# A three-stage attention and feed-forward kernel, rewritten around a list schedule of its own

## The chip, the cores and the metric

The kernel runs as one program on one core of one Trainium2 chip. The metric is the device time of one execution in microseconds (us). A core has five engines that run side by side, each through its own queue in order: TensorE (PE, matrix products, with its weight loads shown as PEld), VectorE (DVE), ScalarE (ACT), GpSimd (POOL) and SyncE (SP, which issues the transfers here).

## The reference

Four batches pass through three stages. All arithmetic is in float32 and the answer must be near a float32 result.

```
A  8 heads of 64; 32 global and 512 local positions (S = 544):
   out_g = softmax(q_g k_all^T / 8) v_all
   out_l = softmax([q_l k_g^T / 8, q_l k_l^T / 8 where |i-j| <= 32]) [v_g; v_l]
   x = heads side by side                                  (544 x 512)
B  4 experts, each a causal attention of one head of 64:
   top 2 of x w_gate, softmax over the two = gate
   out = sum_e gate_e * softmax_causal(x wq_e (x wk_e)^T / 8) (x wv_e) wo_e
C  h = relu(out w_in); c = 3-tap convolution of h along the sequence
   result = (h * sigmoid(c)) w_out                         (544 x 512)
```

(The sequence of stages B and C is the 544 positions; `w_in`, `w_out` and `conv_w` arrive as 64-bit floats that the kernel decodes itself.)

## The kernel before

Where more than float32r's precision is wanted, the kernel splits an operand into a high and a low part (`split`, `sub`, `sub_pool`) and makes three products of them, high by high, high by low and low by high. `wo` is multiplied into `w_in` once (`fold_gen`, L196), so stage C starts from the heads' outputs `oh`, `ol`.

**Stage A** (`stream_a`) takes two heads at a time. K and Q of a head stand on 64 partitions twice; K is split into `k1`, `k2` on POOL (L91, L94) and Q on ACT and DVE (L277, L278). Global scores go over 544 keys (`scores_g`, L291); local scores go by 128 queries against windows of 192 or 224 keys (`scores_l`, L312). DVE adds a mask and takes the maximum (L317), ACT makes the exponential and its sum (L322), DVE the reciprocal, and POOL multiplies the probabilities by it (L91, tile `Pa`). They are transposed on PE (`trans_l`, L346), copied by ACT (L347), and multiplied by V on PE into two halves of 64 output rows (`pv_a`, L361; global queries L371). The result is split into `xh`, `xl`.

**Stage B** (`phase_b`) projects Q, K (L444) and V with the gate's logits (L457), ranks the gates on DVE, then works through eight items (expert pair `p`, query tile `i`): `scores` (L541, and the causal mask as a bf16 product, L543), maximum on DVE (L546), exponential with sum on ACT (L548), scaling on POOL (L555), `trans` (L565, copied by DVE, L567), `pv` (L576). The last 32 queries of all four experts go together (L504, L523, L590).

**Stage C** (`phase_c`) makes `h` by columns of 128 (L621), then relu and the middle tap on ACT (L628, L631, L633), two taps on DVE (L641), tanh on ACT (L644), the product on DVE (L648), a split (L650, L104), and `project` (L661) in three products, 768 matrix products in all.

`decode` turns 64-bit weights into float32 with six DVE instructions of 256 columns for each piece (L110 to L119); there are 16 pieces each of `w_in` and `w_out`.

**What sets the order.** Three generators (A; B; C with the weights) are merged by rates, and the framework's own scheduler reorders the result:

```
merge([stream_a(), stream_b(), stream_c()], [60, 46, 36])
with tile.TileContext(nc, schedule_with_timeline_sim=True) as tc:
```

Of the kernel before, what the change touches and what calls it, by code (L numbers as in the profile page):

```python
# [19 lines left out]
S = SL + SG  # L20
KB = 608
# [5 lines left out]
WIN = [(0, 192), (128, 352), (256, 480), (384, 608)]  # L27

PIECE = [[(0, 128, 0), (128, 64, 1)], [(128, 128, 1), (256, 96, 2)],
         [(256, 128, 2), (384, 96, 3)], [(384, 96, 3), (480, 128, 4)]]  # L30
VCH = [(0, 128), (128, 128), (256, 128), (384, 96), (480, 128)]


def key_of_column():
    cols = [("g", t) for t in range(32)] + [("l", t) for t in range(256)]
    cols += [("g", t) for t in range(32)] + [("l", t) for t in range(256, 512)]
    return cols + [("g", t) for t in range(32)]


def local_mask():  # L40
    import numpy as np
    cols = key_of_column()
    m = np.zeros((128, 4, 224), np.float32)
    for i, (a, b) in enumerate(WIN):
        for c in range(a, b):
            kind, t = cols[c]
            if kind == "g":
                continue
            q = 128 * i + np.arange(128)
            m[:, i, c - a] = np.where(np.abs(q - t) <= 32, 0.0, BIG)  # L50
    return m
# [3 lines left out]
def body(ctx, tc, kq, vA, w_gate, wqk, wv, woT, w_in, conv_w, w_out, cmask, out):  # L55
# [7 lines left out]
    def T(shape, dt, name, bufs=1):  # L63
        return sb.tile(shape, dt, name=name, bufs=bufs)

    def PS(*shape):
        return ps.tile([128] + list(shape), F32, name="s", bufs=5)

    def PO(*shape):
        return ps.tile([128] + list(shape), F32, name="t", bufs=3)  # L70

    NW = 6
    NPA = 3
    LB, LS, L0 = (2, 4, 6), (2, 3, 6, 7, 10, 11), 4

    def W2(dt=F32, n=512):
        w = T([128, S], F32, "w2", NW)[:, :n]
        return w if dt == F32 else w.bitcast(dt)

    def W1(name, dt=F32):  # L80
        w = T([128, 274], F32, name, 3)
        return w if dt == F32 else w.bitcast(dt)

    NG = 8

    def G(name, dt=F32R):
        w = T([128, 272], F32, name, NG)
        return w if dt == F32 else w.bitcast(dt)
# [7 lines left out]
    def split(hi, lo, src, eng, scale=1.0):  # L96
        if eng is act:
            act.activation(hi, src, AF.Copy, scale=scale)
        else:
            scale_pool(hi, src, scale)  # L100
        dve.scalar_tensor_tensor(lo, src, scale, hi.bitcast(F32), op0=ALU.mult, op1=ALU.subtract)  # L101

# [3 lines left out]
    def decode(raw, w, dst=None):  # L106

        lo, up = raw[:, :, 0], raw[:, :, 1]
        t, f1, p, q = W1("hb", I32)[:, :w], W1("cv", I32)[:, :w], W1("hb", I32)[:, :w], W1("cv")[:, :w]
        dve.tensor_scalar(t, up, 3, 0x3FFFFFF8, op0=ALU.logical_shift_left, op1=ALU.bitwise_and)  # L110
        dve.scalar_tensor_tensor(f1, up, -0x40000000, t, op0=ALU.bitwise_and, op1=ALU.bitwise_or)
        dve.tensor_scalar(p, f1, -0x800000, None, op0=ALU.bitwise_and)
        dve.scalar_tensor_tensor(q, lo.bitcast(U32), 2.0 ** -52, p.bitcast(F32), op0=ALU.mult, op1=ALU.mult)
        dve.tensor_tensor(q, f1.bitcast(F32), q, op=ALU.add)  # L114

        e = W1("hb")[:, :w]
        act.activation(e, up.bitcast(F32), AF.Abs)
        dst = q if dst is None else dst
        dve.scalar_tensor_tensor(dst, e, GUARD, q, op0=ALU.is_ge, op1=ALU.mult)  # L119
        return dst  # L120
# [641 lines left out]
```

## Time and profile before

| | |
|---|---|
| time, median of 3 runs | 587.53 us (585.02 to 591.34) |
| span of the profiled execution, first to last instruction | 579.8 us |
| median of the runs less the span | 7.7 us |
| mean granted clock of TensorE over the span | 0.975 |
| busy: PE, PEld, DVE, ACT, POOL | 523.0, 454.3, 429.0, 357.3, 240.0 us |
| moved by DMA | 40.45 MB |

The profile records one execution from its first to its last instruction. The time of that execution as the runs are timed is not recorded beside it; what lies around the span is taken as the 7.7 us of the third row. Matrix products are pipelined and their recorded lengths overlap, so the pace of PE is read from one start to the next, not from busy time.

### The profile page before, as it was taken

The numbers are of one execution on the slowest core, as the hardware profiler recorded it, in microseconds if no ns is written. First come the engines' busy times: TensorE is split into PE (matmuls) and PEld (weight loads), VectorE is DVE, ScalarE is ACT, GpSimd is POOL, SyncE is SP. The second block draws the span as 40 slices with busy tenths as digits, with TensorE's granted clock in tenths as the row PEclk, the third lists the DMA queues.
The fourth block names the chain that finished last, engine by engine and source line by source line (L and its number), as shares of the span: only waits on it lengthen the run. The fifth ranks groups of instructions, "written<-read, shape, count | busy, mean of one in ns | idle before, by whom it ended". The sixth has DMA issues, their size and how long they took to land.

```text
span 579.8 us, 12650 instructions
## 1 busy us (share of the span) xinstructions
PE 523.0 (90%) x4392; PEld 454.3 (78%) x4392; DVE 429.0 (74%) x1316; ACT 357.3 (62%) x1112; POOL 240.0 (41%) x390
## 2 busy tenths in 40 slices
PE   2268888999889698999999999999999999999997
PEld 2157777897667688977777999887879998678997
DVE  4999999767789899869995646656782565485854
ACT  3567767647578567568965566465962663373864
POOL 6758867715666652247465600245402001222000
PEclk9989979999799899999998999999999999999999
DMA  8954444301434450022232400031100000000011
GB/s 215 295 160 112 137 132 111 81 3 42 104 97 128 110 156 1 21 75 52 69 96 56 125 12 2 11 95 53 35 2 20 20 2 21 10 11 11 31 40 38
DMA packets 19855, 40.45 MB, mean 70 GB/s; under 512 B 3408, under 2 KB 8912, under 8 KB 19792
## 3 DMA queue, kind: packets, MB, share of 16 engines
q1 hardware_dynamic: 19792, 39.65, 24.7%
q8 instruction: 34, 0.56, 0.4%
q14 instruction: 29, 0.24, 0.1%
HBM read 35.18 MB, written 4.46 MB: 68 GB/s over the span
## 4 chain that ended last, share of the span: by engine, by line
PE 59%; DVE 17%; DMA 8%; POOL 6%; issue 4%; ACT 3%; SPq 1%; ACTq 0%; POOLq 0%; DVEq 0%
PE s L661 16%; PE s L444 7%; DMA raw<-in_kq_dram 7%; PE s L621 6%; PE s L457 5%; PE t L361 4%; PE s L541 4%; PE t L576 3%; PE t L565 2%; PE s L312 2%; PE t L346 2%; POOL Pa L91 2%; DVE Pa L317 2%; DVE qs L278 2%; DVE cv L114 2%
## 5 line engine op out<-in xcount | busy, mean ns | idle before, releaser
L91 POOL TENSOR_SCALAR Pa<-Pa,ml 128x224 f32<-128x224 f32 (+1 forms) x128 | 70.0, 563 | 29.8 <-DVE ml L326 17.3
L641 DVE SCALAR_TENSOR_TENSOR cv<-hb,cw,cv 128x272 f32<-128x272 f32 x128 | 65.2, 525 | 12.4 <-ACT cv L633 10.8
L661 PE MATMUL s<-gl,wuh 128*128 128x272 f32 x256 | 73.7, 295 | 0.0
L661 PE MATMUL s<-gh,wul 128*128 128x272 f32 x256 | 72.5, 290 | 0.0
L661 PE MATMUL s<-gh,wuh 128*128 128x272 f32 x256 | 70.5, 300 | 0.0
L322 ACT ACTIVATE Pa<-Pa,ml 128x224 f32<-128x224 f32 (+1 forms) x128 | 59.7, 468 | 11.9 <-DVE ml L317 11.7
L555 POOL TENSOR_SCALAR w<-w,stB,gate 128x128 f32<-128x128 f32 (+3 forms) x64 | 45.0, 710 | 53.1 <-DVE stB L553 23.7
L361 PE MATMUL t<-PA,vr 128*64 128x128 f32 (+2 forms) x512 | 52.5, 290 | 2.8 <-ACT PA L347 2.6
L546 DVE TENSOR_REDUCE stB<-s 128x1 f32<-128x128 f32 (+3 forms) x64 | 30.8, 486 | 25.9 <-PE s L543 25.3
L317 DVE CUSTOM_DVE_ANT_0 Pa<-s,lmask 128x224 f32<-128x224 f32 (+1 forms) x128 | 43.9, 373 | 8.1 <-PE s L312 5.2
L347 ACT ACTIVATE PA<-t 128x512 f32<-128x512 f32 x64 | 37.5, 593 | 19.3 <-PE t L346 15.8
L661 PEld LDWEIGHTS s<-gl,wuh 128*128 128x128 f32 x256 | 48.7, 191 | 0.8 <-issue 0.5
L661 PEld LDWEIGHTS s<-gh,wul 128*128 128x128 f32 x256 | 48.5, 190 | 0.0
L661 PEld LDWEIGHTS s<-gh,wuh 128*128 128x128 f32 x256 | 46.4, 191 | 1.6 <-issue 1.2
L361 PEld LDWEIGHTS t<-PA,vr 128*64 128x64 f32 (+2 forms) x512 | 33.5, 138 | 16.2 <-issue 8.3
L346 PE MATMUL t<-ident,Pa 128*128 128x128 f32 x256 | 42.2, 292 | 1.3 <-POOL Pa L91 0.6
L444 PE MATMUL s<-xh,wqkh 128*128 128x272 f32 x128 | 38.7, 302 | 2.6 <-DVE kl L101 1.8
L567 DVE COPY w<-t 128x128 f32<-128x128 f32 (+3 forms) x64 | 30.2, 484 | 14.1 <-PE t L565 13.8
L548 ACT ACTIVATE w<-s,stB 128x128 f32<-128x128 f32 (+3 forms) x64 | 33.0, 522 | 11.8 <-DVE stB L546 7.8
L621 PE MATMUL s<-oh,wfh 128*128 128x274 f32 x128 | 38.9, 304 | 1.0 <-ACT hb L628 1.0
L94 POOL TENSOR_TENSOR k<-raw,k 128x608 fp32r<-128x608 f32 x24 | 38.1, 1586 | 1.4
L312 PE MATMUL s<-k,qs 128*128 128x192 f32 (+1 forms) x208 | 36.0, 306 | 2.5 <-DVE ml L317 2.2
(185 smaller groups left out, 1599.7 us busy)
## 6 DMA issues: line engine op xcount, KB each, us to landing
raw<-in_kq_dram SPq DMA_DIRECT2D x56, 288.0 KB, 4.2
vr<-in_vA_dram SPq DMA_DIRECT2D x16, 320.0 KB, 3.0
out_dram<-w SPq DMA_DIRECT2D x32, 136.0 KB, 1.8
w<-in_w_in_dram SPq DMA_DIRECT2D x16, 256.0 KB, 3.1
w<-in_w_out_dram SPq DMA_DIRECT2D x16, 256.0 KB, 3.9
vB<-in_kq_dram SPq DMA_DIRECT2D x6, 288.0 KB, 4.8
w<-in_wqk_dram SPq DMA_DIRECT2D x4, 256.0 KB, 4.8
w<-in_woT_dram SPq DMA_DIRECT2D x2, 256.0 KB, 5.4
```

The source lines that it names most:

```text
L91: pool.tensor_scalar(dst, src, s, 1.0, op0=ALU.mult, op1=ALU.mult)
L94: pool.tensor_tensor(lo, src, hi.bitcast(F32), op=ALU.subtract)
L312: pe.matmul(t[:, j, :width[i]], qs[:, 128 * i:128 * i + 128], kk[:, a:e], start=(k == 0), stop=(k == 1))
L317: dve.tensor_tensor_reduce(out=Pa[:, i, :w], in0=t[:, j, :w], in1=lmask[:, i, :w], scale=1.0, scalar=3e38, op0=ALU.add, op1=ALU.min, accum ...
L322: act.activation(Pa[:, i, :w], Pa[:, i, :w], AF.Exp, bias=ml[:, i:i + 1], scale=-1.0, accum_out=ml[:, 4 + i:5 + i])
L346: pe.transpose(t[:, 2 * j + p, :], Pa[:, i, c:c + 128], ident)
L361: pe.matmul(o[64 * y:64 * y + 64, i, :], vr[:r, v, 64 * y:64 * y + 64], PA[y, z][:r, 2 * j + p, :], start=(p == 0), stop=(p == 1))
L444: pe.matmul(acc[:, :272], wa[:, c, m], xa[c][:, s], start=(n == 0), stop=(n == 11))
L555: pool.tensor_scalar(PB[y][:, :w], PB[y][:, :w], st[:, 4 + y:5 + y], gate[:, i, 2 * p + y:2 * p + y + 1], op0=ALU.mult, op1=ALU.mult)
L621: pe.matmul(acc[:, :274], a[:, p, 128 * f:128 * f + 128], x[:, p, a0:a0 + 274], start=(k == 0), stop=(k == 5))
L641: dve.scalar_tensor_tensor(cv[:, :N], hb[:, o:o + N], cw[:, k, f:f + 1], cv[:, :N], op0=ALU.mult, op1=ALU.add)
L661: pe.matmul(acc[:, :N], w[:, f, sl], a, start=(f == 0 and k == 0), stop=(f == 7 and k == 2))
```

## The change

Nearly all of `body` is new. The names below are those of the new kernel.

* **An order of its own.** Each piece of work is an `op` with an engine, an assumed length, what it reads and writes, and a due time from a table `PLAN`. `Schedule.run` puts the ops of all five engines into one order (earliest start first, then due time; on PE an op of another tile shape is put back by `HOLD`) and gives out places in a few large tiles (`work`, `xg`, `kq`, `v`, `st`, and the eight PSUM banks `acc`). The framework keeps that order (`tc.manual_schedule`).
* **Stage A by 32 queries.** Each group of 32 local queries meets 128 keys (`local`). Heads are paired on the two halves of the partitions. Q K^T is one float32 product on a tile of 64 rows by 32 columns (512 products, L572), the mask a bf16 product behind each (512, L578), so eight groups share the array. K and Q are no longer split. The global scores use the same tiles (L639).
* **Sums by a column of ones.** V has a 65th column of ones, so P V also gives the softmax sum, and 64 columns are divided behind it (L617). ACT's sums, POOL's scaling of probabilities and the separate mask pass on DVE go; P V is turned round (output rows are queries: 512 products of 32x65, L607; 192, L667; stage B 160 of 128x65, L807), and the result needs another transposition (L625, L820).
* **Stage B** puts the two experts' products side by side on the two row halves (L782) with a mask of half height (L787).
* **Stage C in pairs.** Relu, tanh, product, split, copies and stores take two column blocks (544 columns) at a time; the middle tap goes from ACT to POOL.
* **Decode** takes 512 columns at a time; one of six DVE instructions goes to POOL.

Instructions by engine as ordered: PE products 3736 before (without weight loads), 4692 now; DVE 1316 and 699; ACT 880 and 588; POOL 393 and 255; SP transfers 165 and 97.

The core of the diff:

```diff
-    merge([stream_a(), stream_b(), stream_c()], [60, 46, 36])
+    order = sch.run(trace)
+    with tc.manual_schedule():
+        for o in order:
+            o.fn()
...
+PLAN = {"A": [(0, 26), (26, 75), (75, 170), (170, 265)],
+        "B": [(30, 80), (80, 175), (180, 275), (275, 350)],
...
+                p = c[1].prio
+                if e == "PE" and c[1].mode != mode:
+                    p += self.HOLD
...
+            for t in range(4):
+                for y in range(2):
+                    rows = slice(64 * y, 64 * y + 64)
+                    for g in range(4):
+                        j = 4 * t + g
+                        o = S_[y].ap()[32 * g:32 * g + 32, 128 * t:128 * t + 128]
+                        q = kb.ap()[rows, KB + 32 * j:KB + 32 * j + 32]
+                        pe.matmul(o, q, kb.ap()[rows, 32 * WIN[j]:32 * WIN[j] + 128], start=True, stop=False)
...
+                        pe.matmul(o, quart[rows], am[rows, which[j]], start=False, stop=True)
...
+            op("POOL", .25, lambda y=y: scale_pool(st[y].ap()[:, 4:8], st[y].ap()[:, 0:4], 0.125), r=[st[y]], w=[(st[y], 1)], tag="sclA")
...
+                        pe.matmul(ov()[32 * g:32 * g + 32, y, t], PT[y].ap()[:, 128 * t + 32 * g:128 * t + 32 * g + 32],
+                                  vv[y].ap()[:, 65 * n:65 * n + 65], start=True, stop=True)
...
+                for n, (a, k) in enumerate(((0, 0), (0, 1), (1, 0))):
+                    for y in range(2):
+                        rows = slice(64 * y, 64 * y + 64)
+                        pe.matmul(t.ap()[:, 512 * y:512 * y + w], Q[rows, a, p, qi], K[rows, k, p, :w], start=(n == 0), stop=False)
...
+                        pe.matmul(oe()[:, e], PT.ap()[:, 128 * j:128 * j + 128], vB[:, j, e, :], start=(j == 0), stop=(j == i))
...
+                op("ACT", t_act(544), lambda cv=cv: act.activation(cv.ap()[:, :544], cv.ap()[:, :544], AF.Tanh, scale=0.5), w=ct, tag="tanh")
```

Three places of the order. The first is PE in stage A. Before, where the second pair of heads begins (`s` and `t` are PSUM tiles, `Pg` and `Pa` probabilities):

```order
L291 MATMUL s<-k_121,qs_88 64x272 x2
L335 MATMUL t<-ident,Pg 128x64 x5
L346 MATMUL t<-ident,Pa_82 128x128 x8
L196 MATMUL s<-gl,oh 128x256 x2
L312 MATMUL s<-k_120,qs_88 128x192
L312 MATMUL s<-k_121,qs_88 128x192
L312 MATMUL s<-k_120,qs_88 128x224
```

Now, in the first batch (`acc` is PSUM, `kq` holds K and Q, `work` probabilities, `v` is V with its column of ones, `am` and `quart` make the mask):

```order
L639 MATMUL acc<-kq 32x512 x4
L639 MATMUL acc<-kq 32x192 x4
L594 MATMUL acc<-ident,work 128x128 x12
L654 MATMUL acc<-ident,work 128x128 x6
L607 MATMUL acc<-v,work 32x65 x32
L667 MATMUL acc<-v,work 32x65 x12
L572 MATMUL acc<-kq 32x128 x8
L578 LDWEIGHTS quart
L578 MATMUL acc<-am,quart 32x128
```

Products of one shape now stand in longer runs: eight global score products, 18 transpositions, 44 products of P V, and then a local score group, of whose four blocks the last rows begin the first (eight scores, then eight masks, each with its weight load).

The second place is PE in stage B of the last batch, at the widest query tile (512 keys). Before, one of its four score groups among stage C's products (`gl`, `gh`, `wuh`, `wul`):

```order
L661 MATMUL s<-gh,wuh 128x272
L541 MATMUL s<-kh,qh 128x512
L541 MATMUL s<-kl,qh 128x512
L541 MATMUL s<-kh,qlo 128x512
L543 LDWEIGHTS identb
L543 MATMUL s<-cm,identb 128x128
L565 MATMUL t<-ident,w_7028 128x128 x3
L661 MATMUL s<-gl,wuh 128x272
L661 MATMUL s<-gh,wul 128x272
L661 MATMUL s<-gh,wuh 128x272
```

Now, the score group of two experts (`k`, `q`), ahead of it two transpositions and the last 32 queries' P V:

```order
L867 MATMUL acc<-vB,work 32x65 x20
L800 MATMUL acc<-ident,work 128x128 x8
L877 MATMUL acc<-ident,work 128x128
L782 MATMUL acc<-k,q 128x512 x6
L787 LDWEIGHTS half
L787 MATMUL acc<-cm,half 128x128
```

The score products of two experts stand as one run of six with their masks (four, of which the first is shown) behind. Between matrix products of different tile shapes PE changes 357 times in the order before and 154 times now.

The third place is DVE in the opening. Before, where the first pieces of `w_in` are decoded (`hb`, `cv`):

```order
L110 TENSOR_SCALAR hb<-w_194 128x256
L111 SCALAR_TENSOR_TENSOR cv<-w_194,hb 128x256
L101 SCALAR_TENSOR_TENSOR wqkl<-w_303,wqkh 128x512
L112 TENSOR_SCALAR hb<-cv 128x256
L113 SCALAR_TENSOR_TENSOR cv<-w_194,hb 128x256
L114 TENSOR_TENSOR cv<-cv 128x256
L110 TENSOR_SCALAR hb<-w_307 128x256
L278 SCALAR_TENSOR_TENSOR qs_87<-vB,qs_87 64x544
L119 SCALAR_TENSOR_TENSOR cv<-hb,cv 128x256
L111 SCALAR_TENSOR_TENSOR cv<-w_307,hb 128x256
```

Now (`early` holds the pieces of `w_in`):

```order
L614 TENSOR_SCALAR st<-acc 128x8
L615 RECIPROCAL st<-st 128x8
L617 TENSOR_TENSOR work<-acc,st 128x4x64 x2
L671 TENSOR_SCALAR st<-acc 128x1
L672 RECIPROCAL st<-st 128x1
L674 TENSOR_SCALAR work<-acc,st 128x64 x2
L464 SCALAR_TENSOR_TENSOR early<-early 128x512
L452 TENSOR_SCALAR early<-early 128x512
L582 TENSOR_REDUCE st<-acc 128x4 x2
L337 TENSOR_TENSOR xg<-acc,xg 128x512
L337 TENSOR_TENSOR xg<-acc,xg 64x32 x4
L454 SCALAR_TENSOR_TENSOR early<-early 128x512
L456 TENSOR_SCALAR early<-early 128x512
```

The decode's steps are of 512 columns in place of 256, the addition is no longer among them, and they stand between the first heads' divisions (L614 to L617, L671 to L674) on DVE as before.

## Rows read from the trace of the kernel before

**Rows 1.** The page: its span, and part 1, TensorE's.

```profile
span 579.8 us, 12650 instructions
...
PE 523.0 (90%) x4392; PEld 454.3 (78%) x4392; DVE 429.0 (74%) x1316; ACT 357.3 (62%) x1112; POOL 240.0 (41%) x390
```

**Rows 2.** The page, part 4: the chain that ended last, by engine.

```profile
PE 59%; DVE 17%; DMA 8%; POOL 6%; issue 4%; ACT 3%; SPq 1%; ACTq 0%; POOLq 0%; DVEq 0%
```

**Rows 3.** Windows: length, busy us of each engine (x instructions), granted clock, DMA share, GB/s.

```profile
0.00:30.00 30.00, 8.01 (x36) 7.08 (x37) 21.64 (x41) 12.63 (x29) 20.42 (x34) 1.00 0.95 255
30.00:60.00 30.00, 23.15 (x168) 19.18 (x168) 28.80 (x99) 21.02 (x69) 20.06 (x25) 0.89 0.51 140
60.00:100.00 40.00, 34.39 (x314) 28.93 (x313) 37.68 (x114) 27.66 (x91) 31.19 (x40) 0.91 0.44 124
...
400.00:450.00 50.00, 49.60 (x444) 42.73 (x441) 33.46 (x95) 30.95 (x97) 15.52 (x31) 1.00 0.08 26
```

**Rows 4.** The chain in order of time: start, length, engine, tile, line, instructions.

```profile
537.38 0.88 PE t L565 x8
...
545.70 9.00 PE s L661 x72
...
563.82 11.30 PE s L661 x90
```

**Rows 5.** Timeline of TensorE near 505 and 515 us: start, length to the last end.

```profile
505.30 0.28 PE L621 MATMUL s<-oh,wfl 128*128 128x274 f32 x1
505.52 0.65 PE L576 MATMUL t<-w,vB 128*64 128x128 f32 x6
...
506.32 0.29 PE L621 MATMUL s<-ol,wfh 128*128 128x274 f32 x1
...
515.08 0.50 PE L541 MATMUL s<-kh,qh 64*128 64x512 f32 x1
515.42 0.39 PE L541 MATMUL s<-kl,qh 64*128 64x512 f32 x1
515.65 0.39 PE L541 MATMUL s<-kh,qlo 64*128 64x512 f32 x1
515.97 0.23 PE L543 MATMUL s<-cm,identb 128*128 128x128 bf16 x1
516.04 0.50 PE L565 MATMUL t<-ident,w 128*128 128x128 f32 x3
```

**Rows 6.** Timeline of TensorE from 318 to 323 us.

```profile
318.05 0.78 PE L371 MATMUL t<-PGT,vr 128*64 128x32 f32 x20
318.76 0.46 PE L291 MATMUL s<-k,qs 128*64 128x272 f32 x2
319.05 1.05 PE L312 MATMUL s<-k,qs 128*128 128x192 f32 x8
320.03 0.98 PE L361 MATMUL t<-PA,vr 128*64 128x128 f32 x13
...
320.86 1.14 PE L576 MATMUL t<-w,vB 128*64 128x128 f32 x15
321.93 0.71 PE L291 MATMUL s<-k,qs 128*64 128x272 f32 x4
322.57 0.52 PE L335 MATMUL t<-ident,Pg 64*128 64x64 f32 x5
323.02 1.09 PE L346 MATMUL t<-ident,Pa 128*128 128x128 f32 x8
```

**Rows 7.** Lines by form: busy us, mean ns of one, idle before and its releaser.

```profile
L641 DVE SCALAR_TENSOR_TENSOR cv<-hb,cw,cv 128x272 f32<-128x272 f32 x128 | 65.2, 525 | 12.4 <-ACT cv L633 10.8 <-ACT oh L592 0.3
...
L94 POOL TENSOR_TENSOR k<-raw,k 128x608 fp32r<-128x608 f32 x24 | 38.1, 1586 | 1.4
...
L361 PE MATMUL t<-PA,vr 128*64 128x128 f32 x256 | 44.1, 295 | 2.8 <-ACT PA L347 2.6 <-DMA vr<-in_vA_dram 0.2
...
L104 DVE TENSOR_TENSOR xl<-t,xh 128x512 fp32r<-128x512 f32 x16 | 10.9, 682 | 1.8 <-ACT xh L366 1.7
```

More of the change, by code (lines that the diff above doesn't have):

```diff
@@ new lines, with key_blocks, masks @@
+WIN = [0, 0, 2, 3, 4, 6, 7, 8, 10, 11, 12, 14, 15, 16, 18, 20]
+VW = sorted(set(WIN))
+def key_blocks():
+    out = []
+    for p in range(24):
+        if p % 4 == 0:
+            out.append(("g", 0))
+        elif p == 22:
+            out.append(("l", 14))
+        elif p == 23:
+            out.append(("z", 0))
+        else:
+            out.append(("l", 3 * (p // 4) + p % 4 - 1))
+    return out
+def masks():
+    import numpy as np
+    blocks = key_blocks()
+    found, which = [], []
+    for j, w in enumerate(WIN):
+        q = 32 * j + np.arange(32)
+        m, seen = np.zeros((32, 128), np.float32), set()
+        for c in range(4):
+            kind, t = blocks[w + c]
+            k = 32 * t + np.arange(32)
+            ok = np.zeros((32, 32), bool)
+            if kind == "g":
+                ok[:] = True
+            elif kind == "l":
+                ok = np.abs(q[:, None] - k[None, :]) <= 32
+            assert (kind, t) not in seen
+            seen.add((kind, t))
+            m[:, 32 * c:32 * c + 32] = np.where(ok, 0.0, -BIG)
+        assert (m == 0).sum() == 32 * 32 + sum(min(q1 + 32, SL - 1) - max(q1 - 32, 0) + 1 for q1 in q)
+        for n, f in enumerate(found):
+            if (f == m).all():
+                which.append(n)
+                break
+        else:
+            which.append(len(found))
+            found.append(m)
+    return found, which
@@ L467, in phase_b @@
+        op("POOL", .15, lambda: pool.memset(vB[:, :, :, 64:65], 1.0), r=[("lg", i) for i in range(5)], w=vtok + ["vBone"], tag="one")
+        gate = gates[b % 2]
+        ga, gb = gw
         le = lg[:, :, :, None].to_broadcast([128, 5, 4, 4])
@@ L715, in host_layout @@
+    constants()
+    stage_a(0)
+    fold()
+    constants2()
+    split_weights()
+    conv_load()
+    wout()
+    for b in range(NB):
+        if b:
+            stage_a(b)
+        if b:
+            stage_c(b - 1)
+        stage_b(b)
+    stage_c(NB - 1)
+    order = sch.run(trace)
+    if (tune or {}).get("DRY"):
+        early.close()
+        return sch
+    with tc.manual_schedule():
+        for o in order:
+            o.fn()
+    return sch
 def host_layout(inputs):
```

1343 lines of the change are left out of this document (759 added, 584 removed), and 2 rows, old and new, of the table PLAN.

## The prediction

> **What bounds the kernel now.** I read the page first. TensorE (PE) is busy 523.0 of 579.8 us, the others far less [rows 1], and the chain that ended last runs over PE for 59% of the span and DVE for 17% [rows 2]. The windows say when each counts. In the first 100 us PE is busy 8.01, 23.15 and 34.39 us and issues only 518 of its 4392 products (36, 168 and 314), while DVE is busy 28.80 of 30 us from 30 to 60 and the transfers fill the first 30 us (share 0.95, 255 GB/s). From 400 to 450 PE is busy 49.60 of 50 us [rows 3]. So it is an opening in which PE is starved, and then a long stretch that PE bounds; the last products end at 575.12 us, 4.7 us before the span does [rows 4]. In the long stretch the change is worth what it takes off PE's own time, which I therefore price by kind, from one start to the next.
>
> **Prices on PE.** The big products cost 9.00/72 = 0.125 us and a transposition of 128 columns 0.88/8 = 0.110 us [rows 4]. Plain float32 products go in two passes: L361 shows 256 records of 128 rows for 128 products [rows 7]. From 320.03 to 321.93 us stand 32 such passes of 128 columns (two records are missing): 0.06 us each, though one pass over 128 columns costs a transposition 0.110. So two tiles of 64 output columns run side by side [rows 6]. Passes of 32 columns in L371 cost 0.71/20 = 0.036 us, L312 0.98/8 = 0.122, L291 0.64/4 = 0.160, and a transposition of 64 columns (0.45 less half a shape change)/5 = 0.07 [rows 6]. Score products over 512 columns cost 0.23 us, the mask 0.07. A change of shape: from 505.30 to 506.32 us are two big steps (0.25), eight passes (0.44 at 0.055) and two changes, which leaves 0.165 us for each [rows 5].
>
> **The change part by part, on PE.** Before and after:
> - Big products (1824 at 0.125, and the fold, 96 of 256 columns or 48 of 512): 240 and 239 us. Nothing is gained.
> - Transpositions: 436 x 0.110 and 80 x 0.09 make 55; 464 x 0.110 make 51.
> - Scores of stage A: 128 x 0.160 and 256 x 0.122 make 51. Now there are 64 blocks of eight tiles, each two passes and a mask, 2 x 0.11 + 0.07 = 0.29 us if all eight run together. The trace shows two column tiles together, never two row halves (L541 takes one expert at a time [rows 5]). The ends are 64 x 0.29 = 18.6 us (all together) and 148 (one by one). If the columns go together and the halves do not, it is 37. I take 28, halfway between 18.6 and 37, since column tiles cost nothing where they are shown. The global scores (eight times, four tiles, passes of 512 and 192 columns, 0.59 us a pair) are 9.4 together, 19 with the halves apart and 38 one by one; I take 14. Together 42.
> - P V of stage A: 512 passes x 0.06 and 320 x 0.036 make 42. Now 1024 passes of 65 columns (0.07 each) by four tiles, 18, and 384 by two, 13: 31 in all. Only pairs are shown, so the upper ends are 36 + 13 = 49 in pairs and 99 alone.
> - Scores of stage B: 16 groups of each width, three products (0.23 at 512, less in proportion, not under 0.11) and a mask make 34. Now the same products in pairs and 128 half masks: 39 if the row halves do not overlap, 19 if they do; I take 29.
> - P V of stage B and of the last queries: 320 x 0.06 and 160 x 0.036 make 25. Now 320 x 0.07 (128 rows out, no tiles) and 160/4 x 0.07 make 25. Nothing is gained.
> - Changes of shape: 357 x 0.165 = 59 and 154 x 0.165 = 25.
>
> That is 506 before and 442 now. More than half of the saving of 64 us is the grouping by shape.
>
> **PE's own idle time.** Of the span before, 580 - 506 = 74 us are left. The opening's 518 products are 518/4392 x 506 = 60 us of work in 100, so 40 is lost there; 5 at the end; 29 of the 475 between, or 6%. The opening now: before stage C can use `w_out`, DVE must decode 16 pieces in five steps of 512 columns each, about 0.75 us by L104's 0.682 [rows 7], 60 us; two batches of stage A take it some 36 and stage B's first batch 22, 118 us in all. Two batches of stage A and all weights are about 24 MB, 95 us at 255 GB/s [rows 3]. In these 118 us PE can have the first two batches and part of the third of stage A, the fold and stage B's first batch, 95 to 110 us. I take 24 us lost (10 to 60). For the other 340 us I take 4.5%, 15 us, since the new order knows all engines at once, and 5 at the end. Idle 44.
>
> **The added waits.** Each maximum is now scaled on POOL before ACT can make the exponential (L582, L331, L587). ACT's queue is in order, and behind that exponential stand copies out of PSUM that later products wait for. POOL may be in a subtraction of 512 columns then, 1.3 us by L94's 1.586 for 608 [rows 7]. Twenty such hops lie in the opening: 0 to 26 us, covered by the 24; later POOL has little to do. The halved decode and the paired stage C cost nothing because DVE falls from 429 to about 330 us (128 x 0.525 for L641 [rows 7], 212 of some 512 columns at 0.70, the rest 115) and ACT to about 290, both well under PE.
>
> **Sum.** 442 + 44 = 486 us of span, and the 7.7 us between span and median: 494 us, against 587.53. The span before makes 587.5 in the same way, so the sum stands to the median as it does to the profile.
>
> **Rivals.**
> - *More overlap.* The row halves run side by side and the order holds: scores of A 28 for 42, of B 19 for 29, idle 30 for 44. 494 - 38 = 456. For it: column tiles overlap without loss [rows 6]. Against it: no two row halves in the trace.
> - *A price for each pass.* Small passes cost what L371's do, 0.036 us, whatever runs beside them: 1536 passes and masks of the local scores 55 for 28, 1024 of P V 36 for 18. 494 + 45 = 539. For it: L371's passes are a quarter as long as L361's and cost 0.036 against 0.06 [rows 6]. [...]
> - *The opening and the fixed order.* PE waits 60 us in the opening and 6% later as before: 494 + 36 + 5 = 535. For it: DVE's 118 us, and a granted clock of 0.89 and 0.91 where PE was fed badly [rows 3].
> - *Pairs only.* No more than two tiles together: scores of A 74 + 19 for 42, P V 49 for 31. 494 + 69 = 563.
> - *Slower than before.* The tiles of 64 by 32 run one after another, so that the rewriting does not do what it says: scores of A 148 + 38 for 42, 494 + 144 = 638. It decides from 94 us on: with the global scores as taken, when a block of eight tiles costs 1.9 us and not 0.44 (28/64). Against it: the pairs of rows 6. [...]
>
> **How the numbers follow.** The forecast has 0.42 (470 to 520), more overlap 0.18, a price for each pass 0.15, the opening 0.12, pairs only 0.06, slower 0.05, and 0.02 for no change. A measurement of this kernel can tell about 1% from no change. Faster is the sum of the first five, 0.93; the same 0.02; slower 0.05. The range goes from the best case to just short of pairs only, 455 to 560, and leaves out about 0.15.
>
> **What would show it.** Right: PE's records in runs of one shape; a local score group (L572, L578) in 1.2 to 2.4 us; passes of L607 starting about 0.02 us apart; PE busy in the first 100 us clearly over 65; 80 us less DVE. Wrong: a score group over 5 us (tiles do not overlap); starts of L607 0.036 us apart (a price for each pass); PE waiting for `early`, `work` or POOL's scaled maxima between 20 and 120 us, or a granted clock well under 0.9 there (the opening); long waits of PE for ACT after 150 us (the fixed order). If DVE or ACT, not PE, is on the chain there, the argument from PE's time was wrong.

## The result, and the profile after

| | before | after |
|---|---|---|
| median, us | 587.32 (585.02 to 591.34) | 504.04 (502.97 to 508.95) |
| span of the profiled execution, us | 579.8 | 501.2 |
| TensorE's own time, us | 522.4 | 448.3 |
| pauses of TensorE between its first and last product, us | 44.1 | 43.3 |

The ratio is 0.8608, 95% interval [0.8552, 0.8664]: faster, against a forecast of 494 us in a range of 455 to 560. "Own time" is used below for every kernel: over the records of TensorE, the time from one product's start to the next one's, less the pause between the end of the one and the start of the other, summed by source line. A change of tile shape falls into the line before or behind it. Where an execution took over 1.5% longer than the quickest of its kernel (one of e2_serial, two of e12_maskrow), the times given below leave it out.

The page of after, which answers to [rows 1, 2]: the span, busy times, the queue that brings instructions, and the chain by engine.

```profile
span 501.2 us, 14617 instructions
...
PE 448.6 (90%) x6212; PEld 401.1 (80%) x6212; DVE 309.9 (62%) x699; ACT 258.3 (52%) x588; POOL 120.3 (24%) x252
...
q8 instruction: 49, 0.80, 0.7%
...
PE 65%; DVE 14%; ACT 10%; issue 6%; DMA 3%; POOL 2%; SPq 0%; DVEq 0%; ACTq 0%; POOLq 0%
```

TensorE has the same share of a span that is 78.6 us shorter, and more of the chain, 65% for 59. VectorE lost 119 us, ScalarE 99 and GpSimd 120. The windows, columns as in [rows 3]:

```profile
0.00:30.00 30.00, 19.63 (x604) 14.45 (x604) 14.24 (x34) 18.22 (x42) 10.95 (x27) 1.00 0.89 315
30.00:60.00 30.00, 21.40 (x637) 15.85 (x637) 27.21 (x53) 19.84 (x59) 18.58 (x25) 1.00 0.82 279
60.00:100.00 40.00, 37.39 (x401) 33.65 (x402) 30.21 (x78) 18.39 (x45) 18.05 (x25) 0.91 0.29 99
100.00:150.00 50.00, 39.59 (x513) 31.52 (x512) 36.31 (x76) 29.61 (x66) 16.25 (x20) 0.90 0.37 121
...
400.00:450.00 50.00, 47.81 (x434) 43.09 (x434) 31.20 (x77) 25.10 (x54) 6.20 (x18) 1.00 0.05 18
```

In the first 100 us TensorE is busy 78.4 us where it was 65.6 [rows 3], with the transfers at 315 GB/s in the first 30. But from 100 to 150 us it is busy only 39.59 of 50, and the granted clock is 0.91 and 0.90 of full speed there. Late in the kernel it is nearly the same picture as before, 47.81 of 50.

Timeline of TensorE in after around a local score group, columns as in [rows 6]:

```profile
55.29 0.45 PE L572 MATMUL acc<-kq 64*32 64x128 f32 x16
55.53 0.26 PE L578 MATMUL acc<-am,quart 64*32 64x128 bf16 x8
...
56.45 0.32 PE L578 MATMUL acc<-am,quart 64*32 64x128 bf16 x7
56.70 1.11 PE L607 MATMUL acc<-v,work 128*32 128x65 f32 x64
57.63 0.50 PE L667 MATMUL acc<-v,work 128*32 128x65 f32 x11
62.33 0.96 PE L667 MATMUL acc<-v,work 128*32 128x65 f32 x13 [4.19 <-issue]
```

The score group, four blocks of eight tiles, runs from 55.29 to 56.70: 1.41 us. The 64 passes of L607 start within 0.93 us, 0.0145 apart, where the 32 passes of L361 took 0.06 each [rows 6]. And in the middle of the 24 passes of L667 the engine stands for 4.19 us, for which the profile has no releaser ("issue"). The waits of TensorE in after (line waited for: us in total, times, longest) put that beside the others:

```profile
PE acc L800 <- ACT work L794: 8.1, 9, 3.4
PE acc L572 <- DMA kq<-in_kq_dram: 5.4, 1, 5.4
PE acc L667 <- issue: 4.2, 1, 4.2
PE acc L807 <- ACT work L802: 3.9, 9, 0.8
...
PE acc L578 <- issue: 2.1, 1, 2.1
...
PE acc L607 <- issue: 1.1, 1, 1.1
```

So the gain is TensorE's own time: 74 of the 78.6 us by which the span fell. A part of the 74 may be the granted clock, which stood at 0.50 of full speed for 27 us before and 17 in after, up to the last product: 25.6 us of own time fell into these stretches before, 14.7 in after. Work there takes about 1.9 times as long (in the records of e7 below, passes of L807 start 0.216 us apart at half and 0.112 at full clock: 1.93), so that is, as an estimate, 5 of the 74 us. TensorE's pauses are as long as before; they lie elsewhere. Up to 100 us (with the wait for the first product) they fell from 34.4 to 21.6 us, from 100 to 150 us they rose from 2.0 to 10.4, 5.3 of them where stage B's transpositions (L800) wait for its exponentials, and behind that they stayed at 16.5 and 16.7.

### The profile page after: what moved, and what is told of

Same layout as the page of the kernel before. It is cut to its first block, busy times and chain, and to the rows that moved or that the text cites. A ratio compares the mean times of both kernels' runs of the same rounds, so it can differ in the third digit from the quotient of the medians.

```text
span 501.2 us, 14617 instructions
## 1 busy us (share of the span) xinstructions
PE 448.6 (90%) x6212; PEld 401.1 (80%) x6212; DVE 309.9 (62%) x699; ACT 258.3 (52%) x588; POOL 120.3 (24%) x252
## 3 DMA queue, kind: packets, MB, share of 16 engines
q1 hardware_dynamic: 16272, 42.33, 24.6%
## 4 chain that ended last, share of the span: by engine, by line
PE 65%; DVE 14%; ACT 10%; issue 6%; DMA 3%; POOL 2%; SPq 0%; DVEq 0%; ACTq 0%; POOLq 0%
PE acc L941 18%; PE acc L704 9%; PE acc L807 7%; PE acc L903 6%; PE acc L724 5%; DVE work L918 3%; PE acc L782 3%; PE acc L607 2%; PE acc L800 2%; PE acc L572 2%; ACT work L587 2%; ACT work L910 1%; PE acc L496 1%; PE acc L639 1%; PE acc L667 1%
## 5 line engine op out<-in xcount | busy, mean ns | idle before, releaser
L941 PE MATMUL acc<-xg,wuh 128*128 128x272 f32 x512 | 100.8, 294 | 0.8 <-ACT work L910 0.5
L918 DVE SCALAR_TENSOR_TENSOR work<-work,cw 128x272 f32<-128x272 f32 x128 | 67.7, 546 | 32.7 <-POOL work L331 30.9
L941 PEld LDWEIGHTS acc<-xg,wuh 128*128 128x128 f32 x512 | 80.1, 189 | 2.2 <-ACT work L910 1.0
L941 PE MATMUL acc<-xg,wul 128*128 128x272 f32 x256 | 73.8, 288 | 0.0
L903 PE MATMUL acc<-o,wfh 128*128 128x274 f32 x256 | 51.4, 296 | 1.4 <-ACT work L910 1.3
L704 PE MATMUL acc<-xg,wqkh 128*128 128x272 f32 x256 | 49.8, 292 | 0.0
L941 PEld LDWEIGHTS acc<-xg,wul 128*128 128x128 f32 x256 | 48.2, 188 | 0.0
L807 PE MATMUL acc<-vB,work 128*128 128x65 f32 x320 | 43.4, 278 | 5.0 <-ACT work L802 3.9
L807 PEld LDWEIGHTS acc<-vB,work 128*128 128x128 f32 x320 | 40.0, 194 | 8.8 <-ACT work L802 6.1
L587 ACT ACTIVATE work<-acc,st 128x128 f32<-128x128 f32 x128 | 36.1, 384 | 14.6 <-POOL st L331 13.1
L903 PEld LDWEIGHTS acc<-o,wfh 128*128 128x128 f32 x256 | 40.2, 189 | 2.5 <-ACT work L910 2.0
L800 PE MATMUL acc<-ident,work 128*128 128x128 f32 x160 | 26.2, 284 | 8.2 <-ACT work L794 8.1
L724 PE MATMUL acc<-wvh,xg 128*128 128x260 f32 (+1 forms) x160 | 32.1, 287 | 0.3 <-ACT work L596 0.3
```

The source lines that it names most:

```text
L587: op("ACT", t_act(128, 1, 1), lambda y=y, t=t, sl=sl: act.activation(P[y].ap()[:, sl], S_[y].ap()[:, sl], AF.Exp, bias=st[y].ap()[:, 4 + t ...
L704: pe.matmul(acc.ap()[:, 512 * z:512 * z + 272], wa[:, c, m], xa[:, s], start=(n == 0), stop=(n == 11))
L724: pe.matmul(acc.ap()[:r, :260], x[:, o_ + 128 * i:o_ + 128 * i + r], wa[:, c, :], start=(n == 0), stop=(n == 11))
L800: pe.transpose(tp.ap()[:, 128 * j:128 * j + 128], Pb.ap()[:, 128 * j:128 * j + 128], ident)
L807: pe.matmul(oe()[:, e], PT.ap()[:, 128 * j:128 * j + 128], vB[:, j, e, :], start=(j == 0), stop=(j == i))
L903: pe.matmul(acc.ap()[:, 512 * f:512 * f + 274], a[:, p, sl], O[:, x, p, 270 * z:270 * z + 274], start=(k == 0), stop=(k == 5))
```

## Experiments

Each is one edit of the kernel after, timed against the kernel before on the same chip (585.9 to 589.0 us there). Differences "from after" are between medians, 504.04 us being after's, whose four executions spread from 502.97 to 508.95. "At half" is the time of a profiled execution in which TensorE's granted clock was 0.50 of full speed.

### Do tiles of both kinds run side by side?

**e2_serial** issues a local group tile by tile:

```diff
-            for t in range(4):
-                for y in range(2):
-                    for g in range(4):
...
+            for y in range(2):
...
+                for g in range(4):
+                    for t in range(4):
...
                         pe.matmul(o, q, kb.ap()[rows, ...], start=True, stop=False)
-                for y in range(2):
...
-                    for g in range(4):
...
                         pe.matmul(o, quart[rows], am[rows, which[j]], start=False, stop=True)
```

> The changed kernel with one edit, the order of all else kept: the local scores' products are issued tile by tile (expert half, group, block), each with its mask behind it, so that neighbours in PE's queue belong to the same tile of 64 by 32. Theory (the changed kernel is faster because eight small tiles run together on PE, and PE's own time sets the span): a score group grows from 1.4 us (55.29 to 56.70 us in the changed kernel's trace) to at most 32 x (2 x 0.11 + 0.07) = 9.3 us, sixteen of them: about +110 us (90 to 126). Rival 1 (PE takes tiles out of order, so the order in the queue does not matter): within 5 us. Rival 2 (PE has slack and the gain came from the other engines' shorter work): under +30 us.

Measured: 578.35 us (577.99 to 579.38), ratio 0.9846 [0.9769, 0.9924], 74.3 from after, under the 90 to 126 expected and far over both rivals. Timeline of TensorE in e2_serial, the start of such a group:

```profile
62.06 0.40 PE L572 MATMUL acc<-kq 64*32 64x128 f32 x2 [0.22 <-DVE xg L337]
62.30 0.21 PE L573 MATMUL acc<-am,quart 64*32 64x128 bf16 x1
62.36 0.38 PE L572 MATMUL acc<-kq 64*32 64x128 f32 x2
62.58 0.22 PE L573 MATMUL acc<-am,quart 64*32 64x128 bf16 x1
```

One tile's two passes and its mask now take 0.27 to 0.30 us before its next pair begins, nearly as long as a whole block of eight in after (1.41/4 = 0.35). Own time of the local scores went from 23.8 us (L572, L578) to 114.4, which is 1.79 us for a block of eight. The pauses shrank by 12.6 us, which is why less than the 90.6 arrived in the time. The same instructions in another order give back nearly all of the change's gain: the main theory stands, below its size. The edit also makes score and mask of one tile alternate, but nothing is left for that to cost: one by one they were expected at 2 x 0.11 + 0.07 = 0.29 us. What e2 shows is that the new scores depend on the order of tiles; it does not show that 74 of the 83 us come from the scores of stage A, whose own time fell by 24.6 us from before to after (the table below has the rest).

**e3_halves** keeps the four column tiles together and runs the two row halves one after the other:

```diff
-            for t in range(4):
-                for y in range(2):
...
+            for y in range(2):
...
+                for t in range(4):
                     for g in range(4):
...
```

> The changed kernel with one edit, the order of all else kept: the local scores take one row half (one head) after the other, four blocks each, so that only four column tiles stand next to each other. If the two row halves ran together in the changed kernel, a group grows from 1.4 to 8 x 0.29 = 2.3 us or a little more, sixteen of them: +14 to +18 us. Rival (the halves never overlapped, as no row of the kernel before shows them to): within 3 us.

Measured: 514.76 us, ratio 0.8763 [0.8703, 0.8822], 10.7 from after, under the 14 to 18 expected. Timeline of TensorE in e3_halves, within such a group:

```profile
56.93 0.40 PE L572 MATMUL acc<-kq 64*32 64x128 f32 x8
57.15 0.24 PE L576 MATMUL acc<-am,quart 64*32 64x128 bf16 x4
57.20 0.40 PE L572 MATMUL acc<-kq 64*32 64x128 f32 x8
```

Four column tiles take 0.27 us, as long as one tile alone in e2; all eight take 0.35 in after. Own time of L572 rose from 15.9 to 27.8 us, the masks (L576 here) stayed at 7.9, and the pauses gave 10.7 us back. The other lines' own time rose by 9.5 us, with the clock at half for 48 us against 17 in after. The local scores come to 35.7, next to the 37 of the prediction's "columns together, halves apart". So in after the row halves do run side by side.

### What a mask and a change of shape cost

**e4_masks** makes every mask product of stage A's local scores twice:

```diff
+                        pe.matmul(o, quart[rows], am[rows, which[j]], start=False, stop=False)
                         pe.matmul(o, quart[rows], am[rows, which[j]], start=False, stop=True)
```

> The changed kernel with one edit: every mask product of the local scores is issued twice (the mask counts double, the softmax is the same), 512 products and 512 weight loads more, the order of all else kept. The products themselves: 64 blocks x 0.07 = +4.5 us. Theory of supply (PE's stops inside a group with no wait, 1.07, 2.13 and 4.19 us in the first 60 us, come from instructions that PE has not yet been given while transfers fill the DMA engines): such stops grow in number or length, and the time rises by 8 to 15 us. Rival (the stops have another cause): the stops stay as they are, and the time rises by 3 to 6 us.

Measured: 520.87 us, ratio 0.886 [0.8801, 0.8919], 16.8 from after, above the theory and the rival. The masks' own time rose by only 6.2 us (7.9 to 14.1); some 10 us more stand in other lines (L807's 2.5 the largest), with the clock at half for 41 us against 17. And the waits of TensorE in e4 without a releaser are seven, 10.7 us, where after has three of note and 7.4 (L607 of after is L608 here, L639 is L640):

```profile
PE acc L572 <- issue: 5.0, 4, 1.8
PE acc L608 <- issue: 4.9, 2, 2.8
...
PE acc L640 <- issue: 0.8, 1, 0.8
```

So the stops grew in number and length, as the theory of supply has it, but the time does not follow from them: all pauses together grew by 1.5 us, since others shrank. Of the 18 us that the span grew by, the greater part is other lines' own time, with more of the execution at half clock. The stops are taken up below.

**e6_switch** puts a small product of another tile shape between the two halves of each `h` group of stage C, 64 changes of shape more:

```diff
+                        if f:
+                            pe.matmul(acc.ap()[0:32, 812:876], ident[:, 0:32], ident[:, 0:64], start=True, stop=True)
```

> The changed kernel with one edit: in the middle of each of stage C's 32 groups for h, one small float32 product of 32 output rows is put between two of full shape (its result is not used), so PE changes shape 64 times more (154 to 218), the order of all else kept. Theory (a change of shape costs PE 0.165 us, and PE's time sets the span): 64 x 0.165 + 32 x 0.1 for the product = +11 to +14 us. Rival (the price of a change is hidden behind neighbours, or PE has slack in stage C): under +4 us.

Measured: 519.51 us, ratio 0.8843 [0.8773, 0.8914], 15.5 from after, 1.5 above the theory's upper end, with the clock at half for 31 us against 17. Own time of the lines concerned rose by 13.1 us (51.1 to 56.9, and 7.3 for the new products), 0.41 for each of the 32 insertions. One of them in the timeline of TensorE:

```profile
305.60 0.29 PE L905 MATMUL acc<-o,wfl 128*128 128x274 f32 x1
305.81 0.30 PE L900 MATMUL acc<-ident 128*32 128x64 f32 x2
306.04 0.52 PE L905 MATMUL acc<-o,wfh 128*128 128x274 f32 x2
306.40 0.29 PE L905 MATMUL acc<-o,wfl 128*128 128x274 f32 x1
```

From 305.60 to 306.40 it takes 0.80 us, where three big products at their usual 0.128 take 0.38. In the records the two passes of L900 start 0.08 us apart. At that price they make 0.16 of the 0.42, which leaves 0.13 us for each of the two changes; the prediction's 0.165 would leave only 0.04 for a pass. A change has a price that TensorE pays, then, but some 0.13 us.

### Pairs, and the order's lengths

**e7_nopairs** splits five steps of stage C back into two instructions each, as here:

```diff
-  act.activation(cv.ap()[:, :544], cv.ap()[:, :544], AF.Tanh, scale=0.5)
+  [act.activation(cv.ap()[:, 272 * f:272 * f + 272], cv.ap()[:, 272 * f:272 * f + 272], AF.Tanh, scale=0.5) for f in range(2)]
```

> Stage C's relu, tanh, gate product, rounding and remainder are split back into two instructions of 272 columns each; the order of everything else stays. ScalarE gets about 96 and VectorE about 60 more instructions, at about 0.2 us each 19 and 12 us more busy time. Theory (TensorE's own work is the bound, so pairs in the feed-forward give nothing here): at most 3 us slower than after. Rival (the chain relu, convolution, tanh, product ends in front of TensorE, so the pairs carry part of the gain): 8 us or more slower, with new waits of the feed-forward's second product on VectorE.

Measured: 504.99 us (501.29 to 508.18), ratio 0.8585 [0.85, 0.8671], 1.0 from after, as the theory has it. ScalarE was busy 269.4 us for 258.3, and TensorE's pauses did not grow (39.7 us). These pairs of the feed-forward are worth nothing that shows within the spread of the executions.

**e5_lengths** tells the planner measured lengths:

```diff
-        op("PE", 2.4, scores, r=[kb, "am", "quart"], w=S_, mode="64x32", tag="scoresA")
+        op("PE", 1.4, scores, r=[kb, "am", "quart"], w=S_, mode="64x32", tag="scoresA")
...
-                op("PE", .02 + .115 * (i + 1), pv, ..., mode="f", tag="pvB")
+                op("PE", .02 + .225 * (i + 1), pv, ..., mode="f", tag="pvB")
```

> The list schedule is told the lengths that the trace of after shows on TensorE: a local score group 1.4 us instead of 2.4, its P V 1.0 instead of 1.3, and stage B's P V 0.225 us per key block instead of 0.115. Nothing else is edited; the order of the work moves. Theory (the pauses of TensorE come from the opening, where loads and instruction supply set them, not from a wrong table): idle inside the span stays at 43 us give or take 4, the time within 4 us of after. Rival (the order is off because the lengths are): idle falls by 8 us or more and the time with it.

Measured: 510.46 us, ratio 0.8705 [0.8631, 0.8778], 6.4 above after, more than the 4 us of the theory. The pauses stayed at 43.5 us as the theory says; own time rose by 10 us, with the clock at half for 37 us. Better lengths did not make a better order.

### P V of stage B

**e8_pvtiles** gives both experts' P V of a pair to four column tiles in one group; **e11_pvtiles1** does the same expert by expert:

```diff
-                        pe.matmul(oe()[:, e], PT.ap()[:, 128 * j:128 * j + 128], vB[:, j, e, :], start=(j == 0), stop=(j == i))
+                        [pe.matmul(oe()[32 * g:32 * g + 32, e], PT.ap()[:, 128 * j + 32 * g:128 * j + 32 * g + 32], vB[:, j, e, :], start=(j == 0), stop=(j == i)) for g in range(4)]
```

> Stage B's P V, which takes 0.115 to 0.120 us per pass in after (320 passes, 38 us, where the prediction had 0.07), goes over four column tiles of 32 queries, both experts of a pair in one group; 191 changes of tile shape in place of 153. Theory (a float32 weight load of 128 columns sets the pace of these passes): 1,280 passes at the 0.0145 to 0.02 us that stage A's P V shows take 19 to 26 us, 12 to 19 less, and 38 changes at 0.165 us give 6 back: 6 to 13 us faster than after. Rival (the pace is that of the 65 columns streamed twice, or the tiles wait for one another): no gain in the passes, 6 us or more slower.

> As e8_pvtiles (stage B's P V over four column tiles of 32 queries), but each expert's P V stays a group of its own, as in after, so that none waits for the other expert's probabilities; 200 changes of tile shape in place of 153. Theory (in e8 the passes gained 13.5 us as the trace showed, and waits for both experts' probabilities together gave 8 back): 38 to 25 us of passes, 47 changes at 0.165 us give 8 back, idle stays near 44: 3 to 7 us faster than after. Rival (the waits of e8 come from the order, which any new shape moves): idle at 48 us or more, the time within 3 us of after or above it.

Measured: e8 507.49 us, ratio 0.8652 [0.8584, 0.872], 3.5 above after, where 6 to 13 below were expected; e11 499.67 us (498.67 to 500.4), ratio 0.8522 [0.847, 0.8575], 4.4 below after, within the 3 to 7 expected, and its longest execution is shorter than after's shortest, 502.97. Groups by line and form (busy us, mean ns of one, idle before) of the product and its weight load, in after:

```profile
L807 PE MATMUL acc<-vB,work 128*128 128x65 f32 x320 | 43.4, 278 | 5.0 <-ACT work L802 3.9 <-DVE o L337 0.9
...
L807 PEld LDWEIGHTS acc<-vB,work 128*128 128x128 f32 x320 | 40.0, 194 | 8.8 <-ACT work L802 6.1 <-DVE o L337 1.2 <-issue 0.4
```

and in e11:

```profile
L807 PE MATMUL acc<-vB,work 128*32 128x65 f32 x1280 | 28.0, 225 | 3.7 <-ACT work L802 3.4
...
L807 PEld LDWEIGHTS acc<-vB,work 128*32 128x32 f32 x1280 | 20.7, 111 | 11.0 <-ACT work L802 6.9 <-issue 2.3
```

Own time: 38.4 us (0.120 for each of 320 passes) in after, 24.9 in e8 and 25.3 in e11 (0.020 for each of 1,280). The weight load went from 194 ns for 128 columns to 111 for 32. Both kernels gain the 13 us in these passes; in e8 the pauses rose by 8 to 51.2, in e11 by 4 to 47.6, just under the 48 of its rival. That the load of 128 columns sets the pace fits both, but narrow tiles also run beside one another, and no run parts the two.

### The pauses without a releaser

In the records of TensorE (weight loads and products counted), the three pauses of after stand behind record 699, 1,208 and 2,482: 509 and 5 x 254.8 apart. In e4, with 1,024 instructions more, such pauses stand behind 700, 954, 1,464, 1,973, 2,228 and 2,739: 254 to 255 apart, or twice that. In e6, e7, e9, e10 and e11, which begin with after's order, they stand behind 699, 1,208 and 2,482 again. In e2, where as many instructions are spread over a longer time, there is none. The queue q8 moved 49 packets of 16,384 bytes in after, 53 in e4 (1,024 more), 46 in e12 (768 fewer) and 56 in e11 (1,920 more): one packet more or less for 256 instructions of TensorE in e4 and e12, for 274 in e11. And TensorE goes on 2.4 to 2.8 us after such a packet starts: 15.37 and 18.00, 28.34 and 30.80, 59.87 and 62.33 in after, 15.71 and 18.47, 30.00 and 32.43, 62.81 and 65.24 in e11. So the pause is read here, from the spacing of 254 to 255 records and the packets, as the engine waiting for its next instructions, which come by a DMA queue (q8) as the loads do (q1); no record names what it waits for.

Loads need not be in the way for it. In e8 such a pause, behind record 7,579 (699 + 27 x 254.8), stands where the core moved 4 GB/s and the packet of 230.59 us was the only transfer from 229.5 to 233.5 us. The timeline and the window:

```profile
231.56 0.51 PE L607 MATMUL acc<-v,work 128*32 128x65 f32 x20
233.48 0.94 PE L607 MATMUL acc<-v,work 128*32 128x65 f32 x26 [1.41 <-issue]
...
230.00:234.00 4.00, 2.49 (x144) 1.93 (x130) 3.81 (x10) 2.91 (x6) 0.06 (x1) 1.00 0.02 4
```

The packet before it had started only 3.83 us earlier, at 226.76, and TensorE had started 208 instructions in between.

Two experiments took away loads, one took away instructions. **e9_lessload** and **e10_lessload2** (the name behind # is the run's; its memset stands at the end of a line):

```diff
-        load(raw, lambda: raw.ap()[:, :2 * n].bitcast(I32), bits.bitcast(I32), 2 * n, lead=lead, tag=tag)
+        load(raw, lambda: raw.ap()[:, :64 if spare else 2 * n].bitcast(I32), bits.bitcast(I32)[:, :64 if spare else 2 * n], 2 * n, lead=lead, tag=tag)
...
+    [pool.memset(D_.view(i, 1), 1.0) for i in range(8)]            # e9
+    [pool.memset(D_.view(i, 1)[:, 64:], 1.0) for i in range(8)]    # e10
```

> The eight loads of the feed-forward's first weights bring 64 of 1,024 columns each (the rest of the buffer is set to a constant once at the start by GpSimd), so about 3.9 of the 18 MB that the first 60 us move are gone; TensorE's, VectorE's and ScalarE's instructions and their order are the same, and the folded weights are not the reference's. Theory (TensorE's pauses inside a group, 1.1, 2.1 and 4.2 us at 17, 29 and 58 us, are its own instructions arriving late behind loads): they shrink to under 2 us in all, and with the loads arriving earlier the time falls by 5 to 12 us. Rival (those pauses have another cause): two of the three are still there with their length, and the time moves by less than 4 us, or only by waits for loads that get shorter.

> As e9_lessload (the eight loads of the feed-forward's first weights bring 64 of 1,024 columns, the folded weights are not the reference's), but GpSimd's constant now covers only the other 960 columns, so that the loads don't wait for it: in e9 SyncE's queue stood behind that wait and TensorE lost 6.8 us at 9 us. Instructions and order of TensorE as in after. Theory (pauses inside a group are TensorE's instructions arriving late behind loads): the three of 1.1, 2.1 and 4.2 us come to under 4 us in all, as in e9 (1.3, 1.0 and 1.6), and the time is 3 to 8 us below after. Rival (another cause): over 5 us of such pauses stay, and the time is within 3 us of after.

Measured: e9 512.84 us, ratio 0.8758 [0.8682, 0.8834]; e10 509.19, ratio 0.8682 [0.8627, 0.8737]; 8.8 and 5.2 us above after. The waits of TensorE in e10:

```profile
PE acc L572 <- DMA kq<-in_kq_dram: 5.3, 1, 5.3
PE acc L578 <- DVE quart L397: 4.6, 1, 4.6
...
PE acc L667 <- issue: 3.6, 1, 3.6
```

The three pauses came to 3.9 us in e9 (1.3, 1.0, 1.6) and 5.1 in e10 (0.8, 0.7, 3.6), against 7.4 in after and up to 10.1 in e7 with the same order. The second, 1.6 to 5.2 us in after, e3, e5, e6, e7, e8 and e11, is at 1.0 and 0.7. The time did not follow: TensorE first lost 6.8 us for a load that stands behind the constant that GpSimd writes (e9), and 4.6 us behind a VectorE copy that took 6.38 us in place of 0.43 while GpSimd wrote it (e10; in e9 the same copy took 0.81, so the cause is open). By the numbers set, e9's 3.9 us miss the theory's 2, e10's 5.1 speak for the rival, and neither time is as either had it. The three pauses stand behind the same records in both, which shows the place. Only the second is shorter in both, and TensorE came to it 7 to 8 us later than in after, so whether the loads make these pauses longer is not shown.

**e12_maskrow** leaves 384 mask products out by making each as wide as four; the masks lie in another order for that, copied by three VectorE instructions in place of one:

```diff
+                for g in range(4):
+                    pe.matmul(S_[y].ap()[32 * g:32 * g + 32], quart[rows], am[rows, 128 * g:128 * g + 512], start=True, stop=False)
...
-                        pe.matmul(o, quart[rows], am[rows, which[j]], start=False, stop=True)
```

> In a local score group the eight tiles each take one mask product of 512 columns ahead of the scores, in place of four of 128 columns after them: 128 mask products instead of 512, 768 instructions of TensorE fewer (weights and products), the order of groups nearly that of after. Theory (eight tiles stream beside each other, and what the masks cost beyond that is instructions): 16 groups at 0.21 us of streaming plus some 0.1 us, 5 us instead of 7.9, and less for TensorE's instruction supply to bring: 2 to 6 us faster. Rival (long streams of different tiles run one after another): 128 products at 0.21 us are 27 us, 19 more, and the time is 15 us or more above after.

Measured: 505.62 and 507.25 us, 1.6 and 3.2 above after (all four executions: 510.33, ratio 0.8705 [0.8605, 0.8806]), where the theory had 2 to 6 below and the rival 15 or more above. No run shows the 0.21 us for 512 columns that both are added up from: the score products over 512 columns before stood 0.23 us apart [rows 5]. The waits of TensorE in e12:

```profile
PE acc L801 <- ACT work L795: 8.0, 9, 3.4
PE acc L568 <- DVE quart L397: 4.5, 1, 4.5
...
PE acc L725 <- DVE wfl L337: 3.4, 1, 3.4
PE acc L496 <- POOL xg L334: 2.9, 3, 1.6
PE acc L595 <- DVE xg L337: 2.6, 1, 2.6
...
PE acc L640 <- issue: 0.8, 1, 0.8
```

The masks took 4.2 us for 7.9, 0.033 for each of 128, so these longer streams of different tiles overlapped too, but the scores behind them 2.8 more. Of the pauses without a releaser one of note is left (L640), yet all pauses up to 150 us are 32.1 us as in after (32.0): TensorE now stands for VectorE and GpSimd, which prepare the folded weights (L725, L496) and the outputs of stage A (L595). (The 4.5 us for `quart` lie ahead of the first product, as the 5.4 for `kq` do in after.) What the instructions gave, the opening took.

**e13_both** is e11 and e12 in one:

> e11_pvtiles1 and e12_maskrow in one kernel. Theory (the gains are TensorE's work, and work adds up): scores and masks of stage A 3 us less than in after, P V of stage B 13 less, 47 more changes of shape 8 more, so 442 us of TensorE's own work at most and a time of 494 to 500 us. Rival (what work gives is lost again to waits and half clock, which the order of the opening decides, as in e12): idle of 48 us or more and a time of 500 to 508 us.

Measured: 508.57 us (504.55 to 511.41), ratio 0.8664 [0.8615, 0.8712]. Pauses 50.9 us, own time 448.5 with the clock at half for 31 us: the rival, 0.6 us past the upper end of its time. The version to keep is e11.

## Why the prediction was right, and where its terms were off

The step that carried it held: TensorE's own time bounds the kernel, and it falls by tiles side by side and by fewer changes of shape. The shares came out otherwise, see the third point. The forecast was 506 to 442, measured 522.4 to 448.3. Own time by kind, changes of shape included, before and after, in us:

| kind | predicted, changes apart | measured |
|---|---|---|
| big products | 240, 239 | 260.5, 251.6 |
| transpositions | 55, 51 | 61.9, 62.1 |
| scores of A | 51, 42 | 60.4, 35.8 |
| P V of A | 42, 31 | 57.9, 31.3 |
| scores of B | 34, 29 | 47.1, 26.3 |
| P V of B and last | 25, 25 | 34.6, 41.2 |
| changes of shape | 59, 25 | in the others |

- *Scores of A.* "28, halfway between 18.6 and 37" was too careful: 23.8, and e3 puts the halves-apart case at 35.7. The global scores took 12.0 us for 14: the group at 20.85 us takes 1.31 us, eight of them 10.5, near the 9.4 of all four tiles together and not the 19 with the halves apart.
- *P V of stage B* "320 x 0.07" is the mis-sized term: 0.120 a pass. The 0.07 came from 65 streamed columns alone, but a full-width pass of 65 columns costs about as much here as one of 128 (transpositions 0.110). With 32 columns of weights on four tiles, e8 and e11 got 13 us of it back.
- *Changes of shape* were to be 59 and 25, "more than half of the saving of 64 us". At e6's 0.13 us the 203 changes fewer are worth 26 of the 74 us, an estimate; no run puts the old number of changes back. So the greater part of the gain lies in the products, above all the scores and the P V of stage A and the scores of stage B, 72 us together in the table with the changes among them. That the total came out near is in part luck: the changes were priced too high and the products too low.
- *Half clock* had no term. All prices come from rows at full clock. By the factor of 1.9 above, the 25.6 and 14.7 us of own time in stretches at half clock hold 12 and 7 us that no price has, as an estimate: most of the 16 and all of the 6 us by which the work came out above 506 and 442.
- *Idle 74 to 44* failed. Measured as pauses, with both ends, it is 579.8 - 522.4 = 57 before and 501.2 - 448.3 = 53 after. The 74 was a remainder: 580 less a work of 506 that was priced 16 us too low. In the 118 us of the forecast's opening 27.7 us are lost where it had 24, and behind them 21.0 where "the other 340 us" at 4.5% were to lose 15: the forecast is 4 us short in the one and 6 in the other.
- *The 7.7 us around the span* were 1.8: in after, 502.97 timed for a span of 501.2, and 1.7 to 1.9 in every execution of after and the experiments. By that, the span before came from an execution quicker than each of those timed.

Together: work 6 us above the forecast, idle 9 above, 6 less around the span, which makes 503 for 494; the median, 504.04, lies 1 above the profiled execution. The third cancels one of the first two by luck.

The rivals. *A price for each pass* falls: L607's passes, which go to different tiles, start 0.0145 us apart, under 0.036. *Pairs only* falls with 1.41 us a group. *More overlap* was right in its mechanism (the row halves) and wrong in its idle. *The opening* named where the idle was missed, at 4 us in the opening and 6 behind it rather than 36 and 5. *Tiles one after another* did not occur, but e2 shows that its turning point was well placed: it was to decide at 1.9 us a block, and at 1.79 the kernel is 1.5% faster than before. *The added waits*: ScalarE stood 13.1 us for POOL's scaled maxima (in front of L587), and of that at most 2.8 us reached TensorE (L594 waiting for L587).

What stays open: which of loads, VectorE's decoding and stage B's exponentials sets the 32 us of the first 150 in after. e9, e10 and e12 only show that the pauses without a releaser alone do not. And the same order of TensorE ran between 501.29 and 508.95 us in after and e7, with pauses of 2.1 and 5.2 us at one place in the two executions and the clock at half for 17 and 41 us. One stretch of that, from the windows of e7:

```profile
340.00:358.00 18.00, 16.64 (x80) 14.02 (x81) 8.00 (x21) 8.74 (x24) 0.18 (x1) 0.53 0.00 1
```

TensorE is busy 16.64 of 18 us at 0.53 of its clock, in stage B's products, where after has 1.00 (336 to 354 us). What starts it was not tried. A stretch at half clock near 350 us, 6 to 17 us long, stands in the profiles of e3, e4, e6, e7, e8 and e13 and in no other, so part of what these lie above after may be this and not their edit. In after's own executions the time goes with the granted clock too: 502.97 us at a mean of 0.983, 503.60 at 0.980, 504.47 at 0.979 and 508.95 at 0.966.

## What to carry to other kernels

Small tiles overlapped here where neighbours in the queue went to different tiles (23.8 us of own time for the local scores) and not where they went to the same one (114.4): write the loop over tiles innermost, since the order alone was worth 74 us here. Do not price a pass by its stream alone: a full-width float32 pass cost 0.11 to 0.12 us here whether it streamed 128 columns or 65. Take idle from the pauses in the trace, never as the span less a priced sum. Where short products follow each other closely, count TensorE's instructions too: here it stopped for 0.7 to 5.2 us at multiples of about 255 of its records.

## What the runs showed of the hardware that was not expected

Tiles in the two row halves overlapped as column tiles did: four blocks of eight tiles in 1.41 us, 23.8 us for all local scores, 35.7 with the halves apart and 114.4 one by one. A change of tile shape cost some 0.13 us in e6. TensorE stopped for 0.7 to 5.2 us at multiples of about 255 of its recorded instructions, in after while the core's transfers ran at 279 to 315 GB/s (windows of 30 us), in e8 once at 4 GB/s, and in after and e11 went on 2.4 to 2.8 us after a packet of the instruction queue began. A mask product of 512 columns in eight tiles cost 4.2/128 = 0.033 us each, though the float32r scores over 512 columns before stood 0.23 us apart [rows 5].
